# A mixture-of-experts stage: TensorE's order taken from the program, transposes at fixed places, a GpSimd drain for each expert

## The chip, the core and the metric

One core of one Trainium2 chip runs the whole program. The metric is the device time of one execution in microseconds (us), median of several runs. The engines are TensorE (PE; its weight loads are listed apart as PEld), VectorE (DVE), ScalarE (ACT), GpSimd (POOL) and SyncE (SP, which here only issues DMAs).

## The reference

Three layers follow one another: attention among clustered tokens, a dense MLP, and a mixture of experts over the MLP's output. Only the last layer is touched:

```
def _moe2_ref(x, w_gate, w_noise, noise, w1, w2):       # x: 1536 x 512, E = 8 experts, F = 1024
    noisy_logits = x @ w_gate + log1p(exp(x @ w_noise)) * noise
    top2, top2_w = two largest per token, softmax over the two
    for e in range(E):
        for k in range(2):
            mask = top2[:, k] == e
            h = maximum(x[mask] @ w1[e], 0)
            out[mask] += top2_w[mask, k, None] * (h @ w2[e])
```

## The kernel before

Attention and the MLP take the first two thirds of the time. While the MLP's second half runs (`middle`, line 1237), tokens are routed: each token's row is scattered to a slot list in DRAM, `xs`, one region per expert. Then `moe2` (line 1427) works through the experts in passes. One call of `expert` (line 1380) is one pass over some slots of one expert:

- Pass A is expert 1, first half (240 slots); pass B expert 0, second half; pass C expert 1, second half. (Expert 0's first half is in `middle`.)
- Six passes follow, one for each other expert, in order of load; they are called here by their slots: R432, R416, R408, R400, R392 and R384.

**A pass.** `ffn1` (lines 1320 to 1338) multiplies the first weights with the transposed rows `xT`, 12 matmuls into PSUM bank 0 or 1 for each of eight blocks `fb` of the hidden layer; ACT writes the high part `hh` (relu), DVE the rest `hl`. `ffn2` (line 1340; `ffn2_t`, line 1372, with the operands the other way round) adds that block's share to the pass's accumulators: three matmuls for each of two, three or four banks from bank 2 on. The program's loop is ffn1 one block ahead of ffn2. For the last three blocks (`TAIL`), ffn2 comes at the end, accumulator by accumulator, so that an accumulator is ready after each three groups of three matmuls. This stretch is called the tail: 6 groups with two accumulators, 12 with four.

**The result.** Passes R432 to R392 are "flipped": the accumulators hold the result transposed, ACT and DVE alternately copy them to `yT`, and during the next pass four "back" steps (function `after`) transpose them on TensorE through PSUM banks 6 and 7 in turn; DVE scales them (`put`, line 1358), and POOL scatters them to `out` by an indirect DMA. A pass whose `Y` is true adds to rows that an earlier pass wrote, so POOL clears `Y` and gathers the old rows (`gather_out`, line 1207: a memset and one indirect DMA per accumulator).

**The next pass's rows.** `xpose_part` (line 1226), called four times, transposes a fourth of the next rows `X` into bank 6 or 7 (the two in turn), ACT copies it to `xT` (line 1234), and DVE writes the low part (line 1235). So the third call can't write its bank before ACT and DVE have read the first call's. `meta` (line 1175) works out six small things from `X` on POOL.

**The next weights.** In each pass eight pieces of weights are prepared (`conv`): SP loads a 512 KB piece into one of three buffers `stg`, ACT makes the high part (line 1127), DVE and for some pieces POOL the low part (line 1131); when a piece is done, its buffer takes the piece after next but one. The `step` hook places them: pieces 0 to 7 of a pass after its blocks 0 to 7.

**What sets the order.** The framework's planner orders each engine's queue by its own model of times. `manual_schedule` exempts engines from that: their queue is in the program's order. For `moe2` this is said of ACT and SP (lines 1579 and 1580), and for TensorE only in the tail of the last pass. So in every other place of `moe2`, TensorE's order is the planner's. POOL's and DVE's is the planner's throughout. `last()` in the tail of a pass fetches and transposes the next rows.

Of the kernel before, what the change touches and what calls it, by code (L numbers as in the profile page):

```python
# [14 lines left out]
AF = mybir.ActivationFunctionType  # L15
# [8 lines left out]
DM = H * D  # L24
KB = DM // 128
# [4 lines left out]
FB2 = F2 // 128  # L30
# [4 lines left out]
CH = HALF // 2  # L35
# [10 lines left out]
TAIL = 3  # L46
# [54 lines left out]
PRI = 600  # L101
PRI1 = 600
FX = FB1 - KB
OOB = 1.0e6
TINY = float(2.0 ** ((897 + 128) // 8 - 127) * (1 + ((897 + 128) % 8) / 8))
NP = H // 2
# [508 lines left out]
class Moe:  # L615
# [7 lines left out]
    def consts(self):  # L623
# [27 lines left out]
        nc.vector.memset(z[:, DM + 2:DM + 3], -1.0)  # L651
        nc.vector.memset(z[:, DM + 3:DM + 4], OOB)
        self.zrow = z
# [510 lines left out]
    def gather_half(self, b):  # L1164

        X = (self.rows if b else self.yp).tile([CH, 2, 2, ROW], F32, tag="R" if b else "Y", name="Xh")
        for e in range(2):
# [20 lines left out]
    def gather_rest(self, e, r):  # L1188
# [6 lines left out]
                       allow_small_or_imprecise_dtypes=True)  # L1195
        v.tensor_scalar(sl[:, :, 1:2], sl[:, :, 0:1], t[:, 3:4], OOB, op0=OP.is_ge, op1=OP.mult)
        v.scalar_tensor_tensor(sl[:, :, 1:2], sl[:, :, 0:1], t[:, 0:1], sl[:, :, 1:2], op0=OP.is_lt, op1=OP.mult)
# [9 lines left out]
    def gather_out(self, g):  # L1207
        nc = self.nc
        m, idx = g
        Y = self.yp.tile([m.shape[0], m.shape[1], DM], F32, tag="Y", name="Y")  # L1210
        nc.gpsimd.memset(Y, 0.0)
        for k in range(m.shape[1]):
            nc.gpsimd.indirect_dma_start(
                out=Y[:, k, :], out_offset=None, in_=self.out,
                in_offset=bass.IndirectOffsetOnAxis(ap=idx[:, k, 0:1], axis=0),
                bounds_check=NT - 1, oob_is_err=False)
        return Y

# [121 lines left out]
    def ffn2(self, W, ps, h, fb, ks=None):  # L1340
        nc = self.nc
        hi, lo = W[FB2 + fb]
        hh, hl = h
        for k in range(len(ps)) if ks is None else ks:
            cp = ps[k].shape[0]
            sl = slice(k * cp, (k + 1) * cp)
            for n, (a, w) in enumerate(((hh, hi), (hh, lo), (hl, hi))):
                nc.tensor.matmul(ps[k], a[:, sl], w, start=(fb == 0 and n == 0), stop=(fb == FB2 - 1 and n == 2))

    def combine(self, g, Y):  # L1350
        nc, tc = self.nc, self.tc
# [25 lines left out]
            for n, (w, a) in enumerate(((hi, hh), (lo, hh), (hi, hl))):  # L1377
                self.nc.tensor.matmul(ps[d], w[:, sl], a, start=(fb == 0 and n == 0), stop=(fb == FB2 - 1 and n == 2))  # L1378

    def expert(self, W, xT, g, Y, cp, last=lambda: None, before=lambda: None, final=False, flip=False,  # L1380
               step=lambda i: None):

        nc = self.nc
        ck = xT.shape[3] // cp
        if flip:
            ffn2, ps = self.ffn2_t, [self.bank((2 + d,), [128, ck * cp]) for d in range(KB)]
        else:
            ffn2, ps = self.ffn2, [self.bank((2 + k,), [cp, DM]) for k in range(ck)]
        h = [self.ffn1(W, xT, 0)]
        for fb in range(FB2 - TAIL):  # L1390
            h.append(self.ffn1(W, xT, fb + 1))
            if fb == 0:
                before()
                Y = self.gather_out(g) if Y else None
                if final:
                    self.tc.keep_in_program_order(nc.gpsimd.drain())
            ffn2(W, ps, h[fb], fb)
            step(fb)
        for fb in range(FB2 - TAIL + 1, FB2):
            h.append(self.ffn1(W, xT, fb))  # L1400
            step(fb - 1)
        put = self.combine(g, Y)
        yT = self.xg.tile([128, KB, ck * cp], F32, tag="xU", name="yT") if flip else None
        with self.tc.manual_schedule(engines={mybir.EngineType.PE}) if final else ExitStack():
            for k in range(len(ps)):
                if k == len(ps) // 2:
                    last()
                    step(FB2 - 1)
                for fb in range(FB2 - TAIL, FB2):
                    ffn2(W, ps, h[fb], fb, (k,))  # L1410
                if not flip:
                    put(k, ps[k])
                elif k % 2:
                    nc.vector.tensor_copy(yT[:, k], ps[k])
                else:
                    nc.scalar.activation(yT[:, k], ps[k], AF.Copy)

        def after():
            for k in range(ck if flip else 0):
                pt = self.bank((6, 7), [cp, DM])  # L1420
                for d in range(KB):
                    nc.tensor.transpose(pt[:, d * 128:d * 128 + 128], yT[:, d, k * cp:(k + 1) * cp], self.ident)
                put(k, pt)

        return after

    def moe2(self, W0, W1, xT1, m1):

        nxt = [None, None]
        n, W, X, reg, st = {}, {}, {}, {}, {}  # L1430
        pieces = [(e, s) for e in range(2, E) for s in ORDER]
        count = {"ld": 0, "cv": 0}

        def second():
            nxt[:] = self.gather_half(1)
            self.xpose(*nxt[0][:2], (6, 7))

        def load():
            i = count["ld"]
            if i == len(pieces):  # L1440
                return
            count["ld"] += 1
            e, s = pieces[i]
            if s == ORDER[0]:
                reg[e] = self.nc.values_load(self.ordi[0:1, e - 2:e - 1], engines=(mybir.EngineType.SP,), min_val=2,
                                             max_val=E - 1)
                W[e] = [None] * 8
            st[i] = self.weights_load(s, [w[bass.ds(reg[e], 1)].rearrange("o k n -> (o k) n")
                                          for w in (self.w1, self.w2)])

        def conv():
            i = count["cv"]
            if i == len(pieces):
                return
            count["cv"] += 1
            e, s = pieces[i]
            W[e][s] = self.weights_split(e % 2, st.pop(i), s)
            load()

        def rows(e):  # L1460
            X[e] = self.gather(reg[e], *CAPS[e - 2])

        def turn(e):
            cp, ck = CAPS[e - 2]
            n["xT"] = self.xtile(cp * ck)
            self.xpose(X[e], n["xT"], (6, 7))
            n["m"] = self.meta(X.pop(e)[:, :, DM:], self.ord[:cp, e - 2:e - 1], self.nc.gpsimd)

        def plan(e, at):
            def step(i):  # L1470
                if i == at[0]:
                    rows(e)
                if i in at[1]:
                    conv()
            return step

        def first(i):
            if i == FB2 - 1:
                for _ in range(3):
                    load()  # L1480

        self.expert(W1, xT1, m1, True, CH, second, step=first)
        self.expert(W0, nxt[0][1], nxt[0][2], False, CH, lambda: self.xpose(*nxt[1][:2], (6, 7)),
                    step=plan(2, (4, (3, 5, 7))))
        done = lambda: None
        self.expert(W1, nxt[1][1], nxt[1][2], True, CH, lambda: turn(2), step=plan(2, (None, (0, 2, 3, 5, 6))))
        for e in range(2, E):
            xT, m = n["xT"], n["m"]
            more = e + 1 < E
            done = self.expert([x for p in W.pop(e) for x in p], xT, m, True, CAPS[e - 2][0],  # L1490
                               lambda: turn(e + 1) if more else None, done, not more, more,
                               plan(e + 1, (0, range(FB2))) if more else lambda i: None)

    def rest(self):
# [12 lines left out]
def kernel(ctx, tc, q, k, v, centroids, moe_w_in, moe_w_out,  # L1507
                                                         w_gate, w_noise, noise, w1, w2, out):
    nc = tc.nc
# [40 lines left out]
    def hook(fb):  # L1550
        if fb % 2:
            s["W"] += moe.weights_part(0, 0, fb // 2, (w1[0], w2[0]))
        if 1 <= fb <= NB:
            next(run)
        elif fb == FX:
            s["A"] = moe.gather_half(0)
        if fb >= FX:
            for X, xT, _ in s["A"]:
                moe.xpose_part(X, xT, fb - FX, (0, 1))
        yield  # L1560
# [15 lines left out]
    bctx.close()  # L1576
    moe.wB = pool(ctx, "c_wB", 1)
    W1 = moe.middle(acc, s["W"], *s["A"][0][1:], (w1[1], w2[1]))
    with tc.manual_schedule(engines={mybir.EngineType.Activation, mybir.EngineType.SP}):
        moe.moe2(s["W"], W1, *s["A"][1][1:])  # L1580
    moe.rest()

# [30 lines left out]
```

## Time and profile before

| | us |
|---|---|
| median of 3 runs | 921.78 (921.45 to 922.41) |
| the profiled execution's own time | 922.68 |
| its span, first to last instruction | 920.9 |
| TensorE busy | 881.6 (96%) |
| VectorE busy | 572.5 (62%) |
| ScalarE busy | 487.1 (53%) |
| GpSimd busy | 398.3 (43%) |

Busy time is the union of the engine's instructions as the hardware profiler recorded them. The profiled execution's own time holds 1.8 us that lie outside its span. All time stamps are us from the start of the span.

### The profile page before, as it was taken

The numbers are of one execution on the slowest core, as the hardware profiler recorded it, in microseconds if no ns is written. First come the engines' busy times: TensorE is split into PE (matmuls) and PEld (weight loads), VectorE is DVE, ScalarE is ACT, GpSimd is POOL, SyncE is SP. The second block draws the span as 40 slices with busy tenths as digits, with TensorE's granted clock in tenths as the row PEclk, the third lists the DMA queues.
The fourth block names the chain that finished last, engine by engine and source line by source line (L and its number), as shares of the span: only waits on it lengthen the run. The fifth ranks groups of instructions, "written<-read, shape, count | busy, mean of one in ns | idle before, by whom it ended". The sixth has DMA issues, their size and how long they took to land. (4 is left out here: it accounts for less than half of the span.)

```text
span 920.9 us, 14876 instructions
## 1 busy us (share of the span) xinstructions
PE 881.6 (96%) x5277; PEld 806.0 (88%) x5277; DVE 572.5 (62%) x1129; ACT 487.1 (53%) x1021; POOL 398.3 (43%) x459
## 2 busy tenths in 40 slices
PE   6999999999898999999999999989999999999996
PEld 4898998989887888889998988978879999999995
DVE  3889989998996676676446654652533525445431
ACT  2788888878795565565335444521433324434320
POOL 3134434443565989881000421163432254464631
PEclk9899999999999999999999999999999999999999
DMA  8756765676522333412100340273564455556511
GB/s 216 186 136 181 188 160 163 165 216 180 151 71 101 116 115 115 138 47 69 46 23 24 126 124 23 70 232 115 165 170 128 145 160 168 155 164 198 164 37 65
DMA packets 77531, 120.13 MB, mean 130 GB/s; under 512 B 9858, under 2 KB 55939, under 8 KB 76941
## 3 DMA queue, kind: packets, MB, share of 16 engines
q1 hardware_dynamic: 69997, 100.98, 37.8%
q0 software_dynamic: 7456, 18.16, 6.3%
q8 instruction: 43, 0.70, 0.3%
q14 instruction: 35, 0.29, 0.1%
HBM read 72.85 MB, written 23.76 MB: 105 GB/s over the span
## 5 line engine op out<-in xcount | busy, mean ns | idle before, releaser
L1334 DVE SCALAR_TENSOR_TENSOR hl<-bank,hh 128x240 fp32r<-128x240 f32 (+6 forms) x80 | 40.4, 509 | 138.0 <-ACT hh L1333 138.0
L1333 ACT ACTIVATE hh<-bank 128x240 fp32r<-128x240 f32 (+6 forms) x80 | 35.4, 453 | 169.4 <-PE bank L1325 169.4
L435 DVE TENSOR_TENSOR PTl<-ps_pt,PTh 128x384 fp32r<-128x384 f32 x192 | 98.5, 548 | 12.0 <-ACT PTh L430 11.0
L430 ACT ACTIVATE PTh<-ps_pt 128x384 fp32r<-128x384 f32 x192 | 87.7, 497 | 28.9 <-PE ps_pt L420 27.8
L403 DVE TENSOR_REDUCE nm<-ps_s 128x1 f32<-128x768 f32 x96 | 91.1, 949 | 13.9 <-PE ps_s L398 13.5
L420 PE MATMUL ps_pt<-ident,P 128*128 128x128 f32 x576 | 87.9, 276 | 3.9 <-DVE PTl L435 3.5
L411 ACT ACTIVATE P<-ps_s,nm 128x768 f32<-128x768 f32 x96 | 87.3, 910 | 5.0 <-DVE nm L403 5.0
L1325 PE MATMUL bank<-xT,wB 128*128 128x240 f32 (+3 forms) x480 | 83.7, 321 | 0.0
L420 PEld LDWEIGHTS ps_pt<-ident,P 128*128 128x128 f32 x576 | 68.3, 141 | 13.9 <-DVE PTl L435 10.7
L1325 PEld LDWEIGHTS bank<-xT,wB 128*128 128x128 f32 x480 | 77.2, 192 | 2.2
L823 PE MATMUL bank<-woh,gh 128*128 128x512 f32 x192 | 76.1, 396 | 0.0
L823 PE MATMUL bank<-wol,gh 128*128 128x512 f32 x192 | 75.0, 391 | 0.0
L397 PE MATMUL ps_s<-k,q 128*128 128x384 f32 x192 | 70.7, 368 | 0.7 <-DMA k<-ABk 0.3
L823 PE MATMUL bank<-woh,gl 128*128 128x512 f32 x192 | 69.9, 391 | 0.0
L398 PE MATMUL ps_s<-k,q 80*128 80x384 f32 x192 | 66.7, 347 | 3.1 <-DMA nzt<-in_moe_noise_dram 3.1
L1131 POOL TENSOR_TENSOR wA<-stg,wA 128x512 fp32r<-128x512 f32 x16 | 20.6, 1292 | 107.9 <-DVE wol L715 54.1
L1363 POOL DMA_INDIRECT out_dram<-Y,idx x31 | 35.1, 1133 | 58.6 <-DVE Y L1362 30.0
L455 PE MATMUL ps_o<-PTh,vs 128*128 128x256 f32 x288 | 53.8, 295 | 0.6 <-ACT PTh L430 0.3
L455 PE MATMUL ps_o<-PTl,vs 128*128 128x256 f32 x288 | 53.6, 295 | 0.0
L1325 PE MATMUL bank<-xT,wA 128*128 128x240 f32 (+3 forms) x300 | 51.2, 319 | 0.0
L1378 PE MATMUL bank<-hh,wA 128*128 128x432 f32 (+2 forms) x192 | 50.4, 354 | 0.2 <-ACT hh L1333 0.2
L1325 PEld LDWEIGHTS bank<-xT,wA 128*128 128x128 f32 x300 | 48.0, 189 | 1.4
(311 smaller groups left out, 2301.8 us busy)
## 6 DMA issues: line engine op xcount, KB each, us to landing
stg<-in_moe_w_dram SPq DMA_DIRECT2D x64, 512.0 KB
q<-ABq SPq DMA_DIRECT2D x48, 192.0 KB
k<-ABk SPq DMA_DIRECT2D x48, 192.0 KB
si<-in_moe_w_in_dram SPq DMA_DIRECT2D x14, 512.0 KB
so<-in_moe_w_out_dram SPq DMA_DIRECT2D x14, 512.0 KB
xs<-zrow SPq DMA_DIRECT2D x24, 217.7 KB
ld<-in_k_dram SPq DMA_DIRECT2D x8, 384.0 KB
ld<-in_q_dram SPq DMA_DIRECT2D x8, 384.0 KB
```

The source lines that it names most:

```text
L397: self.nc.tensor.matmul(o, self.g("S1", u, "q")[:, h, qs], self.g("S1", u, "k")[:, h, ks], start=True, stop=False)
L398: self.nc.tensor.matmul(o, self.g("S2", u, "q")[:80, h, qs], self.g("S2", u, "k")[:80, h, ks], start=False, stop=True)
L403: self.nc.vector.tensor_reduce(nm, self.g("s", j)[:, :, :384], axis=AX.XY, op=OP.max, negate=True)
L411: self.nc.scalar.activation(P, self.t.pop(("s", j))[:, :, :384], AF.Exp, bias=self.t.pop(("nm", j)), scale=1.0, accum_out=self.g("sums", u ...
L420: self.nc.tensor.transpose(ps[:, k, :], P[:, k * 128:(k + 1) * 128], self.ident)
L430: self.nc.scalar.activation(self.pt_at(j, g, 0), self.g("pt", j, g), AF.Copy)
L435: self.nc.vector.tensor_sub(self.pt_at(j, g, 1), self.t.pop(("pt", j, g)), f(self.pt_at(j, g, 0)))
L455: self.nc.tensor.matmul(self.g("O", u, qp)[:, h, :], vs[:, h, 2 * i + half].rearrange("p a d -> p (a d)"), PTx[:, kc, :], start=(c == 1 an ...
L823: nc.tensor.matmul(acc[j], g[:, sl], w, start=(fb == 0 and n == 0), stop=(fb == FB1 - 1 and n == 2))
L1325: self.nc.tensor.matmul(ps, w[:, kb, :], xT[:, kb, x], start=(kb == 0 and i == 0), stop=(kb == KB - 1 and i == 2))
L1334: self.nc.vector.scalar_tensor_tensor(hl, ps, 0.0, f(hh), op0=OP.max, op1=OP.subtract)
L1378: self.nc.tensor.matmul(ps[d], w[:, sl], a, start=(fb == 0 and n == 0), stop=(fb == FB2 - 1 and n == 2))
```

## The change

TensorE joins ACT and SP in `manual_schedule` for all of `moe2`, so the places of its instructions in the program become its order. The program is therefore written out more finely. The parts of the next rows' transposes are handed over as a list, and each stands behind a numbered group of the tail (`AT`; pass A has a list of its own, `LATE`). The four back steps of the pass before stand one by one ahead of and behind ffn2 of blocks 0 and 1 (`turn`). `gather_out` is called when the last of them is done; where there are such steps, a `drain` of POOL stands ahead of it. Before, there was one drain, in the last pass, behind `gather_out`. The hook's step 7 comes with the last transposed part, and `meta` ahead of the first. The passes with a drain are R416, R408, R400, R392 and R384.

```
+AT = {2: (1, 2, 3, 4), 3: (), 4: (3, 4, 6, 7)}
+LATE = (3, 4, 5, 5)
...
+        turns = list(before)
+
+        def turn():
+            nonlocal Y
+            if turns:
+                turns.pop(0)()
+            if Y is True and not turns:
+                if before:
+                    self.tc.keep_in_program_order(nc.gpsimd.drain())
+                Y = self.gather_out(g)
+            elif not Y:
+                Y = None
+
         h = [self.ffn1(W, xT, 0)]
         for fb in range(FB2 - TAIL):
             h.append(self.ffn1(W, xT, fb + 1))
-            if fb == 0:
-                before()
-                Y = self.gather_out(g) if Y else None
-                if final:
-                    self.tc.keep_in_program_order(nc.gpsimd.drain())
+            turn()
             ffn2(W, ps, h[fb], fb)
+            turn()
             step(fb)
...
-        with self.tc.manual_schedule(engines={mybir.EngineType.PE}) if final else ExitStack():
-            for k in range(len(ps)):
-                if k == len(ps) // 2:
-                    last()
+        groups = [(k, fb) for k in range(len(ps)) for fb in range(FB2 - TAIL, FB2)]
+        at = at or AT[len(ps)]
+        nxt, n = None, 0
+        for i, (k, fb) in enumerate(groups):
+            ffn2(W, ps, h[fb], fb, (k,))
+            while n < len(at) and at[n] == i:
+                if n == 0:
+                    nxt = last()
+                if n < len(nxt):
+                    nxt[n]()
+                n += 1
+                if n == len(at):
                     step(FB2 - 1)
-                for fb in range(FB2 - TAIL, FB2):
-                    ffn2(W, ps, h[fb], fb, (k,))
...
+        def back(k):
+            pt = self.bank((6, 7), [cp, DM])
+            for d in range(KB):
+                nc.tensor.transpose(pt[:, d * 128:d * 128 + 128], yT[:, d, k * cp:(k + 1) * cp], self.ident)
+            put(k, pt)
+
+        return [lambda k=k: back(k) for k in range(ck if flip else 0)]
...
+        def parts(X, xT):
+            return [lambda kb=kb: self.xpose_part(X, xT, kb, (6, 7)) for kb in range(KB)]
+
         def second():
             nxt[:] = self.gather_half(1)
-            self.xpose(*nxt[0][:2], (6, 7))
+            return parts(*nxt[0][:2])
...
-            self.xpose(X[e], n["xT"], (6, 7))
-            n["m"] = self.meta(X.pop(e)[:, :, DM:], self.ord[:cp, e - 2:e - 1], self.nc.gpsimd)
+            n["m"] = self.meta(X[e][:, :, DM:], self.ord[:cp, e - 2:e - 1], self.nc.gpsimd)
+            return parts(X.pop(e), n["xT"])
...
-        self.expert(W1, xT1, m1, True, CH, second, step=first)
+        self.expert(W1, xT1, m1, True, CH, second, step=first, at=LATE)
...
-    with tc.manual_schedule(engines={mybir.EngineType.Activation, mybir.EngineType.SP}):
+    with tc.manual_schedule(engines={mybir.EngineType.PE, mybir.EngineType.Activation, mybir.EngineType.SP}):
         moe.moe2(s["W"], W1, *s["A"][1][1:])
```

## Rows read from the trace of the kernel before

**Rows 1.** The profile's page, part 1: busy time, share of the span, instructions.
```profile
PE 881.6 (96%) x5277; PEld 806.0 (88%) x5277; DVE 572.5 (62%) x1129; ACT 487.1 (53%) x1021; POOL 398.3 (43%) x459
```
**Rows 2.** Waits of TensorE, 575 to 914 us: total, times, longest.
```profile
PE bank L1232 <- DMA Xh<-xs: 4.3, 1, 4.3
PE bank L1232 <- DMA X<-xs: 1.9, 1, 1.9
PE bank L1325 <- ACT xT L1234: 1.5, 1, 1.5
PE bank L1348 <- ACT hh L1333: 0.2, 1, 0.2
```
**Rows 3.** Stretches behind two long waits; PEclk, the granted clock, is third from the end.
```profile
622.80:626.20 3.40, 3.40 (x15) 3.13 (x14) 0.00 (x0) 0.13 (x1) 2.91 (x6) 0.50 1.06 312
762.80:766.10 3.30, 3.30 (x13) 3.13 (x12) 1.19 (x3) 1.37 (x4) 0.00 (x0) 0.50 0.57 157
```
**Rows 4.** TensorE in order of time: start, duration, what, [idle before <-releaser].
```profile
604.09 1.08 PE L1348 MATMUL bank<-wB,hh 128*120 128x512 f32 x4
...
605.47 1.50 PE L1325 MATMUL bank<-xT,wB 128*128 128x240 f32 x12
606.81 1.10 PE L1348 MATMUL bank<-wB,hh 128*120 128x512 f32 x4
...
622.24 0.53 PE L1232 MATMUL bank<-ident,Xh 120*128 120x120 f32 x3 [4.32 <-DMA Xh<-xs]
...
686.14 0.90 PE L1232 MATMUL bank<-ident,X 104*128 104x104 f32 x8 [1.85 <-DMA X<-xs]
686.82 1.09 PE L1378 MATMUL bank<-hl,wA 128*128 128x432 f32 x4
687.71 4.04 PE L1325 MATMUL bank<-xT,wg 128*128 128x432 f32 x12
...
698.65 2.52 PE L1325 MATMUL bank<-xT,wA 128*128 128x432 f32 x12
...
785.70 2.40 PE L1325 MATMUL bank<-xT,wA 128*128 128x408 f32 x12
787.93 0.53 PE L1378 MATMUL bank<-hh,wA 128*128 128x408 f32 x2
...
790.15 2.38 PE L1325 MATMUL bank<-xT,wA 128*128 128x408 f32 x12
```
**Rows 5.** ScalarE in order of time, at the ends of passes R416 and R408.
```profile
759.22 1.15 ACT L1127 ACTIVATE wA<-stg 128x512 fp32r<-128x512 f32 x2 [6.14 <-DMA stg<-in_moe_w_dram]
...
799.56 1.16 ACT L1127 ACTIVATE wB<-stg 128x512 fp32r<-128x512 f32 x2 [3.88 <-DMA stg<-in_moe_w_dram]
...
801.01 0.89 ACT L1234 ACTIVATE xT<-bank 128x400 fp32r<-128x400 f32 x2
```
**Rows 6.** GpSimd in order of time, passes R416 (first row) and R408.
```profile
738.60 0.31 POOL L1180 TENSOR_SCALAR m<-X,ord 102x4 f32<-102x4 f32 x1 [8.19 <-DMA X<-xs]
...
780.52 1.34 POOL L1363 DMA_INDIRECT out_dram<-Y,idx  x1 [0.30 <-DVE hl L1334]
...
784.12 1.81 POOL L1211 MEMSET Y<- 102x2048 f32 x1 [0.92 <-DMA out_dram<-Y,idx]
...
791.89 1.30 POOL L1131 TENSOR_TENSOR wx<-stg,wx 128x512 fp32r<-128x512 f32 x1
```
**Rows 7.** DMAs issued by SP, in order of time.
```profile
726.04 0.32 SPq L1161 DMA_DIRECT2D X<-xs  x1
...
793.21 0.37 SPq L1118 DMA_DIRECT2D stg<-in_moe_w_dram  x1
```
**Rows 8.** By line: the one drain; the gathers' time to landing; the last gather.
```profile
L1396 POOLq DRAIN  x1: 9335/9335/9335, 896.7 to 896.7; - x1
...
DMA to landing us min/median/max: 3.3/4.0/5.9
...
898.48 1.00 POOL L1213 DMA_INDIRECT Y<-out_dram,idx  x1 [0.30 <-issue]
```

More of the change, by code (lines that the diff above doesn't have):

```diff
@@ L1378, in ffn2_t, with expert @@
                 self.nc.tensor.matmul(ps[d], w[:, sl], a, start=(fb == 0 and n == 0), stop=(fb == FB2 - 1 and n == 2))
-    def expert(self, W, xT, g, Y, cp, last=lambda: None, before=lambda: None, final=False, flip=False,
-               step=lambda i: None):
+    def expert(self, W, xT, g, Y, cp, last=lambda: [], before=(), final=False, flip=False,
+               step=lambda i: None, at=None):
         nc = self.nc
@@ L1401, in expert @@
             step(fb - 1)
+        assert not turns
         put = self.combine(g, Y)
         yT = self.xg.tile([128, KB, ck * cp], F32, tag="xU", name="yT") if flip else None
-        with self.tc.manual_schedule(engines={mybir.EngineType.PE}) if final else ExitStack():
-            for k in range(len(ps)):
-                if k == len(ps) // 2:
-                    last()
-                    step(FB2 - 1)
-                for fb in range(FB2 - TAIL, FB2):
-                    ffn2(W, ps, h[fb], fb, (k,))
[L1411 to L1425, printed above, removed]
+        groups = [(k, fb) for k in range(len(ps)) for fb in range(FB2 - TAIL, FB2)]
[10 more added lines that the diff above has]
+                if n == len(at):
+                    step(FB2 - 1)
+            if fb < FB2 - 1:
+                continue
+            if not flip:
+                put(k, ps[k])
+            elif k % 2:
+                nc.vector.tensor_copy(yT[:, k], ps[k])
+            else:
+                nc.scalar.activation(yT[:, k], ps[k], AF.Copy)
+        def back(k):
[4 more added lines that the diff above has]
+        return [lambda k=k: back(k) for k in range(ck if flip else 0)]
     def moe2(self, W0, W1, xT1, m1):
@@ L1480, in first @@
                     load()
-        self.expert(W1, xT1, m1, True, CH, second, step=first)
-        self.expert(W0, nxt[0][1], nxt[0][2], False, CH, lambda: self.xpose(*nxt[1][:2], (6, 7)),
+        self.expert(W1, xT1, m1, True, CH, second, step=first, at=LATE)
+        self.expert(W0, nxt[0][1], nxt[0][2], False, CH, lambda: parts(*nxt[1][:2]),
                     step=plan(2, (4, (3, 5, 7))))
-        done = lambda: None
+        done = ()
         self.expert(W1, nxt[1][1], nxt[1][2], True, CH, lambda: turn(2), step=plan(2, (None, (0, 2, 3, 5, 6))))
@@ L1490, in moe2 @@
             done = self.expert([x for p in W.pop(e) for x in p], xT, m, True, CAPS[e - 2][0],
-                               lambda: turn(e + 1) if more else None, done, not more, more,
+                               lambda: turn(e + 1) if more else [], done, not more, more,
                                plan(e + 1, (0, range(FB2))) if more else lambda i: None)
```

## The prediction

> **What bounds the kernel now.** I read the busy times first: TensorE is busy 96% of the span [rows 1]. In the expert passes that hides two things: the waits of TensorE, and the speed at which it runs behind them. So the second view is the waits of TensorE from pass A to the end of the last pass [rows 2]. Four kinds are long enough to count, and three of them are single waits: 4.3 us for the rows `Xh`, 1.9 us for the rows `X`, 1.5 us for `xT` from ScalarE. The rest is 0.2 us apiece. The third view is the granted clock behind them [rows 3]: after the first and the third wait it stands at 0.50, the 1.2 GHz level, for about 3.4 us, with TensorE busy all the time. Behind the second, twelve matmuls take 4.04 us where the same twelve take 2.52 in the same pass later [rows 4], so that one is slowed too. Half speed for 3.4 us costs 1.7 us. The short waits of 0.2 us have no such stretch that I count.
>
> Where the waits stand is seen in TensorE's queue in order of time [rows 4]. At 617.92 (622.24 less 4.32) the planner has put transposes of the next rows ahead of pass A's last ffn1 block; the rows land 4.3 us later, while that block and six groups, which need no new rows, stand behind them. At 684.3 it has put R416's transposes at the start of R432, a whole pass early. Both are faults of order alone. The third is not: there ScalarE itself waited 6.14 us for a weight piece [rows 5], and everything in its fixed queue behind that, `xT` too, came late. R408's end shows the same, 3.88 us, with no wait of TensorE at that place.
>
> **The change part by part.** *Added and removed work.* TensorE has the same matmuls and transposes; ACT, DVE and SP the same instructions. Four drains are added on POOL, and one is moved. So the sum consists of waits.
>
> *First wait.* In the program's order TensorE goes on at 617.92 with ffn1 of block 7, 1.34 us (605.47 to 606.81), then four groups; two groups take 1.38 (604.09 to 605.47), so four take 2.76 [rows 4]. The first transpose is reached at 622.02, the rows are there at 622.24: 0.2 us remain of 4.32, and I take it that the clock holds, as I see no slow stretch behind waits of 0.2. The parts that follow lie behind groups 4 and 5, as 240 columns on ACT and DVE need less time than a group and its transposes. Saved: 4.1 + 1.7. SP's fetch of `Xh` moves in the program, but SP has nothing else to issue in between, so it keeps its time.
>
> *Second wait.* R416's rows have landed by 686.14, and their transposes now stand in R432's tail, nearly 30 us later. Saved: 1.85 + 1.7.
>
> *Third wait and the tails of R416, R408, R400 and R392.* Saved if nothing takes its place: 1.5 + 1.7. But now the third part of the transposes stands in the tail behind group 6, and its bank is free only when ACT and DVE have read the first part. ACT's copy stands behind piece 6 of the weights, and that piece's load goes out when POOL has finished piece 3, which it does behind `gather_out` [rows 6, 7]. So I follow one such pass, R408's size, from its start. One ffn1 block takes 2.23 us, ffn2 of four groups 2.22 (785.70, 787.93, 790.15), eight transposes 0.68 [rows 4], so one back step 0.34. The last back step ends after five blocks and four steps: 11.1 + 1.4 = 12.5. Its put and hand-over are 1.0 (an estimate: two ACT passes over 512 columns take 1.16 [rows 5]). The last scatter starts at 13.5; the memset came 3.6 later (780.52 to 784.12), POOL's low part 7.8 after that, and takes 1.3 [rows 6]: 26.2. From the issue of the load to ScalarE's start is 6.35 (793.21 [rows 7] to 799.56 [rows 5]); from there to `xT` 1.45 [rows 5]; reading the first part to the end about 1.05 (half of 0.89, and as much again for DVE): 35.05. TensorE comes to the third part after thirteen blocks, four back steps, seven groups and two parts: 28.9 + 1.4 + 3.9 + 0.7 = 34.9. So it waits some 0.15 us. The chain is that much earlier than in before because there the last scatters stood behind `meta`, and `meta` waited for `X`: 8.19 us in R416 [rows 6].
>
> *The drain.* It stands on POOL between the last scatter and the memset; behind it wait the memset, the gathers, POOL's low parts, thereby SP's loads and ScalarE. The memset waits for the scatter's landing anyhow, so a drain that only waits for landings costs nothing. The one drain of before is on record with 9.34 us from 896.7, to 906.0; the last gather ahead of it was issued at 898.48 and landed, by the median of 4.0, at 902.5 [rows 8], so it held POOL 3.5 us beyond. Bounds: nothing and 3.5 us for each pass. That drain was the first, behind 79 indirect transfers; a new one comes behind eight since the last drain. Taken by transfers, 3.5 x 8 / 79 is 0.35. I take that, as the gathers themselves follow one another without such holds. So three passes (R408, R400, R392) wait 0.15 + 0.35 each: 1.5 together. In R384 no transposes and no weight pieces follow, and its gathered rows are first used at the end of the pass, so its drain is covered there.
>
> The Trainium skill has a rule against this reading: "Perfetto Trace Analysis", section "Sequencer-only Instruction (DRAIN, etc)", says that the profile's record of a drain is its execution alone, without any wait for semaphores ahead of it. By it the whole 9.34 us would be the drain's own, four times on this chain, and the time about 940. The trace does not bear that out as a price: a gather starts at 898.48, inside the drain's record.
>
> *R416.* It has the first drain, and the slowest rows: 12.6 us from issue (726.04 [rows 7]) to landing (738.60 [rows 6]). The fetch comes about 1.5 us into the pass (an estimate: it stands in SP's queue behind the load that follows piece 7, now prepared with the last transposes). If the planner leaves `meta` ahead of the last two scatters, the last one starts at 1.5 + 12.6 + 1 + 1.4 = 16.5, not 13.5: 3.0 us more, and 1.7 for the clock. So between 0.5 and 5.2; neither is nearer to a row, and I take the middle, 2.9.
>
> **Sum.** 922.68, the profiled execution's own time, less 6.0 (first), 3.55 (second) and 3.2 (third) is 909.9. Back come 0.2, 1.5 and 2.9: 914.5. The runs' median lies 0.9 below that execution: 913.6.
>
> **The rivals.** *A new wait in place of the old.* The planner may leave POOL's chain as late as it was. Then the first part is read 2.5 us after piece 6 is begun: at 761.7 in R416, 802.1 in R408 [rows 5]. Five groups (2.8) before the tails' ends, about 759.7 and 802.0, TensorE stands before the third part: waits of 4.8 and 2.9, and R400's I take as R408's. That is 10.6 and three times 1.7, so 909.9 + 0.2 + 15.7 - 0.9 = 924.9. For it: ACT's queue is the same as before, and POOL's is still the planner's. Against it: the scatters no longer have to stand behind late rows, as these are fetched sooner. *Slower by the drain.* If each drain holds POOL its full 9.3, the memset comes 5.7 later than 3.6 in four passes: each waits about 5.9 and loses 1.7, 30 in all: about 940. The drains and their waits eat the whole gain from 1.4 us of wait a pass on (12.5 / 4, less 1.7). For it is the one record; against it that its gathers ran inside. *Part of the gain.* All four tails wait about a microsecond, with half speed behind: 909.9 + 0.2 + 4 x 2.7 - 0.9 = 920.0.
>
> **How the numbers follow.** A measurement of this kernel tells 0.2%, 1.8 us, from no change. Forecast 0.60, with a range of its own from 908.8 (no new waits, 909.9 - 0.9, rounded down) to 917.5 (two tails at their upper bounds); part of the gain 0.12; the new wait 0.16; the drain 0.12. Faster: all of the first and two thirds of the second, 0.68. Same: the rest of the second and half of the third, 0.12. Slower: 0.20. The range from 908.8 to 925 leaves out the drain's case and a little at either end.
>
> **What would show it.** In the new profile the waits for `Xh` and `X` should be gone from TensorE's list (0.2 at most for `Xh`), with the half-speed stretches at 623 and 688. At the ends of R416 to R392 the transposes should stand as four parts between groups, with a short wait or none ahead of the third. On POOL the scatters should come before `meta`, and each drain should end within half a microsecond of the last scatter's landing. I am wrong if ScalarE still waits 4 us or more for piece 6: then TensorE waits for `bank` in the tails, and if the drains reach microseconds past the landings, all of it turns to a loss.

## The result: 0.8% slower, and the profile after

The changed kernel takes 929.0 us (median of 12 runs, 923.43 to 932.06), the kernel before 921.05 on the same chip (12 runs, 917.14 to 923.91). The ratio is 1.0081, 95% interval 1.0062 to 1.0101. The forecast was 913.6 with a range up to 925: wrong in sign.

The profiled execution took 930.48 us, its span is 928.6. The page's first part and the waits of TensorE, 575 to 925 us, answer [rows 1] and [rows 2]. The columns of the second are total, times, longest.

```profile
PE 879.4 (95%) x5277; PEld 802.3 (86%) x5277; DVE 571.7 (62%) x1129; ACT 488.4 (53%) x1021; POOL 393.3 (42%) x459
```
```profile
PE bank L1234 <- DVE xT L1237: 8.6, 5, 3.9
PE bank L1350 <- ACT hh L1335: 7.0, 1, 7.0
PE bank L1380 <- ACT hh L1335: 0.3, 1, 0.3
PE bank L1380 <- DVE hl L1336: 0.3, 1, 0.3
```

Up to line 1390 every line stands two further down than before: transposes are L1234, ACT's and DVE's parts of `xT` L1236 and L1237, ffn1 L1327, ffn2 L1350 and L1380, the put L1364. TensorE's busy time is what it was. The waits for `Xh`, `X` and `xT` from ScalarE are gone, as the change meant. In their place stand waits for a bank that DVE's low part of `xT` has not yet read, and one wait of 7.0 us for ScalarE's `hh` in pass A. Their sum is 16 us, where before had 8.

TensorE in order of time shows the three long ones, which answer [rows 4]: in pass A, at pass A's end, and ahead of the third part in R408's tail.

```profile
619.06 1.21 PE L1350 MATMUL bank<-wx,hh 128*120 128x512 f32 x2 [7.02 <-ACT hh L1335]
...
634.28 0.42 PE L1234 MATMUL bank<-ident,Xh 120*128 120x120 f32 x2 [1.81 <-DVE xT L1237]
...
801.36 0.93 PE L1234 MATMUL bank<-ident,X 100*128 100x100 f32 x4 [3.95 <-DVE xT L1237]
```

Stretches behind the first and the last of them, as [rows 3] (granted clock third from the end): 1.2 GHz again, 0.50 of full speed.

```profile
619.10:622.40 3.30, 3.30 (x10) 2.68 (x10) 2.50 (x22) 0.17 (x1) 0.00 (x0) 0.50 0.15 25
...
801.40:806.70 5.30, 5.30 (x20) 5.08 (x21) 2.66 (x5) 2.44 (x5) 1.03 (x1) 0.50 0.33 102
```

The five drains, by line, answer [rows 8]: minimum, median and maximum, first and last start.

```profile
L1399 POOLq DRAIN  x5: 3606/5006/7826, 734.0 to 898.7; - x5
```

### The profile page after: what moved, and what is told of

Same layout as the page of the kernel before. It is cut to its first block, busy times and chain, and to the rows that moved or that the text cites. A ratio compares the mean times of both kernels' runs of the same rounds, so it can differ in the third digit from the quotient of the medians.

```text
span 928.6 us, 14870 instructions
## 1 busy us (share of the span) xinstructions
PE 879.4 (95%) x5277; PEld 802.3 (86%) x5277; DVE 571.7 (62%) x1129; ACT 488.4 (53%) x1021; POOL 393.3 (42%) x459
## 5 line engine op out<-in xcount | busy, mean ns | idle before, releaser
L1327 PE MATMUL bank<-xT,wB 128*128 128x240 f32 (+3 forms) x480 | 79.7, 318 | 0.0
L1327 PEld LDWEIGHTS bank<-xT,wB 128*128 128x128 f32 x480 | 75.9, 189 | 1.8
L1380 PE MATMUL bank<-hh,wA 128*128 128x432 f32 (+2 forms) x192 | 54.3, 365 | 0.0
L1327 PE MATMUL bank<-xT,wA 128*128 128x240 f32 (+3 forms) x300 | 50.8, 320 | 0.0
L1327 PEld LDWEIGHTS bank<-xT,wA 128*128 128x128 f32 x300 | 47.8, 189 | 1.3
```

Source lines behind the costliest of these rows:

```text
L1327: self.nc.tensor.matmul(ps, w[:, kb, :], xT[:, kb, x], start=(kb == 0 and i == 0), stop=(kb == KB - 1 and i == 2))
```

## The experiments

### Both kernels once more: what belongs to the kernel and what to one execution

The 7.0 us looked odd: TensorE had ended the block that `hh` reads 9.3 us before ScalarE began it, and no other wait stood in ScalarE's queue. So the changed kernel was run again unchanged (`e1_again`), and later the kernel before (`e8_before_again`).

> The changed kernel as it is, once more. In its first profile TensorE waits 7.0 us in pass A for ScalarE's hh of block 5, though TensorE had ended that block 9.3 us earlier and no other wait stands in ScalarE's queue; records of DMA landings are thin there. Theory 'the order makes it': the wait comes from the new order and stands in every execution; then it is here again at about 7 us, and TensorE's waits from 575 us on sum to about 16 us. Rival 'of that one execution': the wait is gone or elsewhere, the waits sum to about 9 us, and the time of the profiled execution is below 925 us. In either case the tails of R416, R408, R400 and R392 wait for the bank of the third part by about 1, 4, 1.4 and 0.5 us.

> The kernel before as it is, once more, for a second trace: the waits for Xh (4.3), X (1.9) and xT (1.5) should stand at the same places, each with a stretch of half clock, if they belong to the kernel and not to the one execution shown.

`e1_again`: 926.56 us against 918.16 of the kernel before on that chip, ratio 1.0093 (1.0057 to 1.0129); profiled 927.09, span 925.3. `e8_before_again`: one run of 917.46 us, span 915.6. The waits of TensorE in the changed kernel, then in the kernel before:

```profile
PE bank L1234 <- DVE xT L1237: 11.7, 4, 6.1
PE bank L1380 <- DVE hl L1336: 1.0, 1, 1.0
```
```profile
PE bank L1232 <- DMA Xh<-xs: 3.9, 1, 3.9
PE bank L1232 <- DMA X<-xs: 1.5, 1, 1.5
PE bank L1325 <- DVE xT L1235: 0.3, 1, 0.3
PE bank L1348 <- ACT hh L1333: 0.2, 1, 0.2
PE bank L1378 <- ACT hh L1333: 0.2, 1, 0.2
```

Neither theory for the changed kernel held whole. The wait for `hh` is gone, so it is not a part of every execution (what caused it stays open). But the wait at pass A's fourth part, 1.81 us in the first trace, is now 6.15 (630.34). In the kernel before, the wait of 1.5 us for `xT` is not there the second time. Its median was 921.05 us beside the first trace and is 917.15 on the chip of the second, so whether the first trace's extra waits belong to one execution or to its chip is not shown. Granted clocks: three stretches of the kernel before (behind `Xh`, behind `X`, and R408's start, whose counterpart in [rows 3] has 0.50), then two of the changed kernel (behind 6.15 us in pass A, behind 2.84 in R408).

```profile
622.10:624.90 2.80, 2.80 (x12) 2.60 (x13) 0.00 (x0) 0.00 (x0) 2.60 (x8) 0.50 1.06 240
686.00:689.40 3.40, 3.40 (x22) 3.28 (x22) 0.00 (x0) 0.00 (x0) 3.21 (x8) 1.00 0.43 151
...
757.50:760.90 3.40, 3.40 (x23) 3.07 (x22) 2.17 (x5) 1.49 (x5) 0.58 (x1) 1.00 0.46 164
```
```profile
630.40:636.50 6.10, 6.10 (x28) 5.99 (x29) 1.67 (x4) 1.08 (x3) 2.10 (x2) 0.50 0.23 63
800.40:803.80 3.40, 3.40 (x14) 3.18 (x13) 2.03 (x4) 2.36 (x5) 0.30 (x1) 0.50 0.58 159
```

These two traces (of two chips) account for the loss. Waits: 11.7 + 1.0 against 3.9 + 1.5 + 0.3 + 0.2 + 0.2, 6.6 us more. Half speed: 6.1 + 3.4 against 2.8 us, of which half is lost, 3.3 more. Together 9.9 us; the spans differ by 9.7 (925.3 less 915.6).

### Pass A: a put in DVE's queue

In `e1_again` pass A's end reads so on TensorE, DVE and GpSimd:

```profile
623.82 0.37 PE L1234 MATMUL bank<-ident,Xh 120*128 120x120 f32 x2
630.34 0.66 PE L1234 MATMUL bank<-ident,Xh 120*128 120x120 f32 x2 [6.15 <-DVE xT L1237]
```
```profile
622.82 0.41 DVE L1237 TENSOR_TENSOR xT<-bank,xT 128x240 fp32r<-128x240 f32 x1 [2.88 <-ACT xT L1236]
629.22 0.75 DVE L1364 SCALAR_TENSOR_TENSOR Y<-bank,m,Y 120x512 f32<-120x512 f32 x1 [5.99 <-DMA Y<-out_dram,idx]
629.88 0.40 DVE L1237 TENSOR_TENSOR xT<-bank,xT 128x240 fp32r<-128x240 f32 x1
```
```profile
622.75 0.94 POOL L1213 MEMSET Y<- 120x1024 f32 x1
...
624.04 1.15 POOL L1215 DMA_INDIRECT Y<-out_dram,idx  x1 [0.19 <-POOL m L1186]
625.50 1.09 POOL L1215 DMA_INDIRECT Y<-out_dram,idx  x1 [0.30 <-issue]
```

The fourth part needs the bank of the second. DVE's low part of the second needs 0.40 us, but in DVE's queue, which is the planner's, the put of the first accumulator stands ahead of it. That put adds to gathered rows `Y`, which land at 629.1. So DVE stands for 5.99 us, and TensorE behind it. The Trainium skill says of it ("PSUM — Partial Sum Buffer", section "Engine vs sequencer instructions") that the queues of ScalarE, VectorE and GpSimd are strict FIFO; the trace agrees, with a ready 0.40 us instruction behind a waiting one for 6 us.

In the kernel before (`e8_before_again`) the same put waits for the same rows, at 629.93. But there the planner had ordered two low parts ahead of it, and it filled TensorE's time with tail groups and with the next pass's ffn1:

```profile
626.52 0.71 DVE L1235 TENSOR_TENSOR xT<-bank,xT 128x240 fp32r<-128x240 f32 x2
629.93 1.56 DVE L1362 SCALAR_TENSOR_TENSOR Y<-bank,m,Y 120x512 f32<-120x512 f32 x2 [2.69 <-DMA Y<-out_dram,idx]
```

Three runs test this: the planner's order in pass A alone (`e2_passA`), the gathers sooner (`e6_gather_first`), and the put later (`e7_put_last`). Their edits, shortened:

```
e2  -    with tc.manual_schedule(engines={PE, Activation, SP}):
    +    with tc.manual_schedule(engines={Activation, SP}):      # in moe2, from pass B on: {PE}
e6  +        with self.tc.manual_schedule(engines={mybir.EngineType.Pool}):
                 self.expert(W1, xT1, m1, True, CH, second, step=first, at=LATE)
e7  +        if at is LATE:                                       # the tail of pass A
    +            stack.enter_context(self.tc.manual_schedule(engines={mybir.EngineType.DVE}))
             ...
    +            if at is LATE: held.append(k)                    # in place of put(k, ps[k])
             ...
    +        for k in held:                                       # behind groups and parts
    +            put(k, ps[k])
```

> The changed kernel, but TensorE's order is the planner's in pass A, and the program's from pass B on. If the first wait of the changed kernel (7.0 us in pass A, and 1.8 for the fourth part) is made by the program's order there: the old wait for Xh of about 4.3 us with 1.7 for the clock comes back in its place, some 4.5 us less in all, about 924.5. If the 7.0 us belong to one execution and not to the order: the old wait comes back for the 1.8 us alone, 4 us more, about 933.

> The changed kernel with GpSimd too in the program's order during pass A: memset and gathers of the old rows Y stand ahead of meta, which waits for Xh. In pass A's tail TensorE waits 6.2 us for the bank that DVE's low part reads, DVE stands in the put, and the put waits 6.0 us for these gathers. If the gathers' late start is the cause: memset at about 620.3 instead of 622.8, the rows 2.5 to 3.7 us sooner, the wait 6.2 falls to 2.5 to 3.7, and with less at half clock some 3 to 5 us off. If the wait has another cause (the part's place), it stays at 6 us.

> The changed kernel with DVE's two puts of pass A behind the four low parts of xT (DVE in the program's order in that tail). If DVE's order is what turns the late gathers into a wait of TensorE: the wait of 6.2 us for the fourth part goes; pass B starts its two blocks of ffn1 (2.9 us), and then ffn2 waits about 2.5 us for the accumulator that the put frees at about 630. So 3.5 us less, and 1 to 2 for the clock. If the low parts wait for something else, the 6 us stay.

`e2_passA`: 927.58 us, ratio 1.0104 (1.0068 to 1.0139), no different from `e1_again`: the wait for `Xh` is back (4.5), the 6.15 gone. Expected were 924.5 or 933, so neither came. The time does not tell what pass A's order alone is worth: in this trace pass A loses less than in `e1_again` (waits of 4.5 and 0.5 and 1.7 for half speed, against 6.15 and 3.1), but R416's third part waits 4.3 where `e1_again` has 1.5.

`e6_gather_first`: 925.46, ratio 1.0077 (1.0058 to 1.0096). The first gather was issued at 622.82, 1.2 us sooner, and the put still waited to 629.25; TensorE's wait was 6.7. That GpSimd's order makes the rows late has fallen, as far as 1.2 us can tell: 2.5 were meant, but the memset had to wait for the scatters ahead of it. The gathers took 6.3 and 5.7 us from issue to landing, where `e1_again` has 5.0 and 4.3.

```profile
621.57 0.96 POOL L1213 MEMSET Y<- 120x1024 f32 x1 [4.46 <-DMA out_dram<-Y,idx]
622.82 1.12 POOL L1215 DMA_INDIRECT Y<-out_dram,idx  x1 [0.30 <-POOL Y L1213]
```

`e7_put_last`: 920.04 against 917.15, ratio 1.0040 (1.0018 to 1.0061), 0.53% below `e1_again`, and 5.4 us below `e6_gather_first` on the same chip. It is the largest single piece of the loss, and it goes by one engine's order alone. The low parts now run as the parts come, the put waits from then on, and TensorE waits for it only at pass B's first ffn2, by 3.0 us where 2.5 were expected:

```profile
PE bank L1234 <- DVE xT L1237: 4.5, 3, 2.8
PE bank L1350 <- DVE Y L1364: 3.0, 1, 3.0
```

### The drains

Edits: `if before:` ahead of the drain becomes `if final:` (`e3_no_drains`); a drain ahead of `gather_out` in the kernel before, in the same five passes (`e4_drains_only`).

> The changed kernel with the drain in the last pass alone; GpSimd's queue is else the same. Theory 'the drains': in the changed kernel the drains end 5.9, 5.4, 4.8 and 4.4 us after the issue of the last scatter in R416 to R392, where the memset of before starts 3.6 after it; without them the memset, the low parts, SP's loads and ScalarE come 2.3, 1.8, 1.1 and 0.8 us earlier and the waits of the third parts shrink by as much, from 1.0, 4.0, 1.4 and 0.5 to 0, 2.2, 0.2 and 0: 4 us less, and 1.7 to 2.7 for the clock if R408's wait becomes short, so 923 to 925. Rival 'the places of the parts': the tails wait since the parts stand too early, with drains or without; the memset waits for the last scatter's landing anyhow, the waits stay within 0.5 us, and so does the time, 929.

> The kernel before with the drains alone: one ahead of gather_out in R416 to R384, the planner's order of TensorE kept (GpSimd's first low part of a pass moves from ahead of the memset to behind it). Theory 'the drains': the chain from the last scatter to ScalarE's piece 6 is 1 to 2 us longer in each pass, plus 1.3 for the low part; R416's wait for xT grows from 1.5 to 3 to 5 us, R408 gets a wait of up to 3 us, so 923 to 929. Rival 'the places of the parts': drains alone are covered, since the planner sets the transposes at the end of the tail: within 1 us of before, 921 to 922.

`e3_no_drains`: 924.11 where `e1_again` has 926.56, ratio 1.0061 (1.0039 to 1.0082). `e4_drains_only`: 922.38 where the kernel before has 918.16, ratio 1.0049 (1.0031 to 1.0068); in its trace R416's wait for `xT` is 3.1 us, R408 and R400 get 0.4 and 0.8. (Its profiled execution took 926.89 us, the slowest of the twelve.) So the drains cost 2.5 us in the changed kernel and 4.2 alone, where each pass's first low part of GpSimd (1.3 us) also moved behind the memset. The 4.2 are clear of no change; the 2.5 are less so, as the intervals of `e3_no_drains` and `e1_again` overlap, and in the trace the tails' waits fall only from 6.5 to 5.3 us, R408's not at all (3.7). That the drains are covered has fallen; that they are the main cause too. From the last scatter's issue to the memset, in us:

| | R416 | R408 | R400 | R392 | R384 |
|---|---|---|---|---|---|
| before (`e8_before_again`) | 3.2 | 3.5 | 5.0 | 3.8 | 3.1 |
| changed (`e1_again`) | 6.3 | 5.6 | 5.1 | 4.3 | 3.6 |
| changed, one drain in R384 (`e3_no_drains`) | 4.2 | 5.5 | 4.5 | 3.9 | 7.5 |

These differences hold more than the drain, since the last scatter takes 3.0 to 5.4 us to land, by pass and run. Its landing is in the trace too, and from there to the memset it is, in us:

| | R416 | R408 | R400 | R392 | R384 |
|---|---|---|---|---|---|
| before (`e8_before_again`), no drain between | 0.1 | 0.1 | 0.1 | 0.1 | 0.1 |
| changed (`e1_again`), a drain in each | 2.1 | 0.6 | 0.6 | 0.6 | 0.6 |
| before with drains (`e4_drains_only`) | 2.1 | 0.6 | 0.6 | 0.6 | 0.6 |
| changed, one drain in R384 (`e3_no_drains`) | 0.1 | 0.1 | 0.1 | 0.1 | 4.5 |

So a drain that follows another by one pass adds about 0.45 us, R416's, the first, 1.9, and R384's, where it is the only one, 4.3.

### The tails: two fixed places

R408 in `e1_again`, ahead of the third part. GpSimd, SP, ScalarE, and TensorE:

```profile
775.50 1.00 POOL L1365 DMA_INDIRECT out_dram<-Y,idx  x1 [0.39 <-DVE Y L1364]
781.14 1.82 POOL L1213 MEMSET Y<- 102x2048 f32 x1 [4.65 <-DMA out_dram<-Y,idx]
782.92 1.36 POOL L1133 TENSOR_TENSOR wB<-stg,wB 128x512 fp32r<-128x512 f32 x1
...
790.48 1.29 POOL L1133 TENSOR_TENSOR wx<-stg,wx 128x512 fp32r<-128x512 f32 x1
```
```profile
791.80 0.37 SPq L1120 DMA_DIRECT2D stg<-in_moe_w_dram  x1
```
```profile
797.14 1.15 ACT L1129 ACTIVATE wB<-stg 128x512 fp32r<-128x512 f32 x2 [4.39 <-DMA stg<-in_moe_w_dram]
...
798.58 0.89 ACT L1236 ACTIVATE xT<-bank 128x400 fp32r<-128x400 f32 x2
```
```profile
799.74 0.56 PE L1234 MATMUL bank<-ident,X 100*128 100x100 f32 x4 [2.84 <-DVE xT L1237]
```

It is the chain that the prediction followed, later by 3 us. In `e8_before_again` the planner put the third and fourth parts where TensorE waited for neither, within the next pass's first block, which needs them last:

```profile
796.73 0.54 PE L1325 MATMUL bank<-xT,wB 128*128 128x400 f32 x2
797.11 0.51 PE L1232 MATMUL bank<-ident,X 100*128 100x100 f32 x4
797.39 1.34 PE L1325 MATMUL bank<-xT,wB 128*128 128x400 f32 x6
798.57 0.51 PE L1232 MATMUL bank<-ident,X 100*128 100x100 f32 x4
```

`e5_later_parts` moves the two parts four groups back:

```
-AT = {2: (1, 2, 3, 4), 3: (), 4: (3, 4, 6, 7)}
+AT = {2: (1, 2, 3, 4), 3: (), 4: (3, 4, 10, 11)}
```

> The changed kernel with the third and fourth part of the transposes behind groups 10 and 11 of a four-bank tail instead of 6 and 7. In the kernel before, the planner had let these parts slip behind the whole tail of R408, into the next pass's first block, which needs them last. If the fixed places 6 and 7 make the waits of the tails: the waits of about 1, 1.4, 2.8 and 1.3 us (once more run) shrink by the four groups, 2.2 us, to near nothing, R408's to at most 1; about 0.5 us a pass comes back as a wait for xT in the next block; 5 us less with the clock, some 921 against 926.5 on the same chip. If they only move: the tails' sums stay within 1 us, and so does the time.

925.02 us, ratio 1.0076 (1.0054 to 1.0098). In the trace R408's wait of 2.8 became 0.7 (for `hl`), but R416's became 1.1 + 0.3 + 2.7; the tails' sum is 5.8 us against 6.5, within the 1 us of the rival. The places alone give at most 1 or 2 us, which these intervals do not tell from nothing, and less than I expected. A part that stands later also delays what is behind it: piece 7, SP's next load, and with it the next fetch of `X`, which in R416 is issued 3.9 us into the pass where `e1_again` has 1.4.

### Taken together

> Two edits together: pass A's puts behind the low parts, and the drain in the last pass alone. If pass A's put and the drains are two separate causes, their gains add: 6.5 and 2.5 us off the changed kernel, 917.5, the time of the kernel before. If both act through the same wait, no more than the 920.0 of the first alone.

> The same two edits, and the third and fourth parts behind groups 10 and 11. Theory 'the fixed places are the third cause': the tails' waits of 1.0, 2.8 and 0.7 us in R416, R408 and R400 go but for about 0.5 each, 2 to 3 us less and 1.7 for the clock where R408's wait was followed by half speed: 913 to 915.5. Rival 'they only move' (in the run with later parts R416's wait grew from 1.0 + 1.5 to 1.1 + 2.7, with the rows X fetched later): within 1 us of the run with two edits.

> The three edits, and pass A's three weight loads (512 KB each) issued ahead of the fetch of Xh instead of behind it. With GpSimd's gathers of Y moved 1.2 us forward they landed no sooner; if that is because the weights' transfers run at the same time, then now Y lands 2 to 3 us sooner, and the wait of ffn2 for the put in pass B (3.0 us) shrinks by as much. If the gathers' 4 to 5 us are their own, the wait stays at 3 us. The price may be a later Xh: the scatters ahead of it share the queues with the weights.

> The three edits (without the loads), and the fetch of the next rows X one place earlier in SP's queue, ahead of the load that follows piece 7 of the pass before. In the changed kernel GpSimd's meta, ahead of three of the four scatters, waits 3.4, 2.0, 0 and 0.9 us for X in R416 to R392. If meta's wait sets when the scatters end, and so the memset, the low parts and ScalarE's piece 6: the waits of meta go, R416's tail gets 1 to 3 us of room, and the time falls by up to 2 us. If the landing of the scatters or the loads sets it: no change.

The kernel before has 917.81 beside these. `e9_put_last_no_drains` (the edits of e7 and e3): 917.11, ratio 0.9993 (0.9976 to 1.0009). The two causes add, and with both taken away the change is worth nothing: in this trace TensorE still waits 4.8 us in the tails and 2.9 for the put, where the kernel before waited 3.9 for `Xh` and 1.5 for `X`. `e10_and_later_parts` (with e5's too): 917.84, 0.9998 (0.9984 to 1.0013), the rival's outcome. `e11_loads_ahead` (`first` loads at `i == FB2 - 2`): 916.62, 0.9993 (0.9976 to 1.0010); the put's wait went, and a wait of 3.3 us for `Xh`, issued at 621.30 instead of 616.8, came in its place. The gathers did land faster: from issue to landing, in `e10_and_later_parts` and then in `e11_loads_ahead`:

```profile
DMA to landing us min/median/max: 4.7/5.0/5.3
DMA to landing us min/median/max: 3.5/3.7/3.8
```

So over 1 us of their time came from the loads beside which they ran. The last three scatters into `xs`, which the fetch of `Xh` waits for, paid for it: they took 7 to 8 us to land, where `e10_and_later_parts` has 3.2 to 3.7. They do not stand in the loads' queue, as the expectation had it (the profile lists q0 for GpSimd's transfers and q1 for SP's); it gives both as a share of the same 16 DMA engines.

`e12_rows_ahead` fetches `X` ahead of piece 7's load:

```
-        def plan(e, at):
+        def plan(e, at, ahead=E):
             def step(i):
                 if i == at[0]:
                     rows(e)
+                if i == FB2 - 1 and ahead < E:
+                    rows(ahead)
                 if i in at[1]:
                     conv()
```

(In its calls, `ahead` is the pass after the next.) 914.83 us, ratio 0.9978 (0.9965 to 0.9992): the only version that beats both kernels, the one before by 0.2%. `X` is issued 0.3 us into R416, where `e10_and_later_parts` had 3.9. `meta` still waits 8.1 us for it, so the expectation that its waits go was wrong, but it starts 4 us earlier in the pass. TensorE's waits are down to these:

```profile
PE bank L1350 <- DVE Y L1364: 3.0, 1, 3.0
PE bank L1380 <- DVE hl L1336: 0.9, 1, 0.9
PE bank L1234 <- DVE xT L1237: 0.7, 1, 0.7
```

## Why the prediction was wrong

**First wait (6.0 us saved): this step failed.** It said that the parts lie behind groups 4 and 5, "as 240 columns on ACT and DVE need less time than a group and its transposes". That was right as far as it goes (ACT's copy takes 0.37 us, DVE's low part 0.40). What stood between them on DVE was not looked at: the put, and behind the put the gathers. The old wait of 4.3 us lay in front of a later one for rows that land at about 629 in either order. In place of 4.3 + 1.7 the changed kernel has 6.15 + 3.05 (`e1_again`). No rival had this place; the one of a new wait in place of the old had only the tails, at 4.8, 2.9 and 2.9 us where `e1_again` has 1.5, 2.8 and 1.3 ahead of the third parts.

**Third wait (3.2 us) and the clock behind the second (1.7): these stood in one trace of two.** The prediction took them from the profiled execution and corrected only by 0.9 to the median. In the second trace of before neither is there: 1.5 us of wait for `X` at full clock, none for `xT` from ScalarE. Of the 12.75 us of saving (6.0 + 3.55 + 3.2), 4.9 (3.2 + 1.7) were not there to save in the second trace.

**Second wait (1.85):** right; it is gone in both traces of the changed kernel.

**R408's tail (0.15 + 0.35): mis-sized by 2.3.** From the pass's start (761.35 in `e1_again`) the last scatter came at 14.2, not 13.5; the memset 5.6 later, not 3.6 + 0.35, as the scatter took 5.1 to land, not 3.4; the low part 9.3 after that, not 7.8, as the pass's first low part had moved between. It ended at 30.4 instead of 26.2 + 0.35. A shorter load gave 1 us back (5.3 from issue to ScalarE, not 6.35). TensorE reached the third part at 35.5 (predicted 34.9) and waited 2.84, and half speed behind it cost 1.7 more, for which the sum had nothing. R416's 2.9 was about right in size (2.4 in `e1_again`, but only 1.5 of it ahead of the third part; 1.0 is ffn2's wait for `hl`), R400's 0.5 is 1.25.

**The drains (0.35 each): nearly right in R408, R400 and R392** (0.45 each, by the landings), and 1.9 in R416, which the prediction had left inside R416's own bounds. The Trainium skill's rule in "Perfetto Trace Analysis", section "Sequencer-only Instruction (DRAIN, etc)", that a drain's record is its execution alone, does not give its price here: the records are 5.0 us in the median, but each begins ahead of the last scatter's and holds the wait for its landing, and removing four of them gave 2.5 us in all.

**What would have shown it** was named rightly for the tails (waits for `bank`), and not for pass A.

## What to carry to other kernels

A wait removed is worth the distance to the next one, so ask of each engine that serves the moved work what stands in its queue between the pieces, and what that waits for: here a put on DVE, whose rows landed 6 us later, undid a saving that TensorE's queue alone seemed to promise. When one engine's order is fixed by hand and the order of the engine that serves it is left to a planner, the two can come to stand against each other; `e7_put_last` took away over half of the loss with DVE's order alone. And a saving read from one profiled execution is worth checking in a second: over a third of this one was not in the second.

## What the runs showed that I had not expected

- A drain's price grew with the indirect transfers issued since the last one: the memset starts 0.6 us behind the last scatter's landing with eight or nine of them, 2.1 with 42 or 43 (R416), 4.5 with 75 (R384 of `e3_no_drains`), and 0.1 without a drain.
- A wait of the same length is followed by half speed in one run and not in another. In R408 2.84 us of wait is followed by 0.50 for 3.4 us in `e1_again`; behind 2.84 us at the same place in `e7_put_last` the clock is 1.00:

```profile
794.70:798.10 3.40, 3.40 (x22) 3.17 (x23) 2.67 (x5) 2.31 (x5) 0.18 (x1) 1.00 0.60 159
```
- In the first trace of the changed kernel ScalarE began `hh` 9.3 us after TensorE's last matmul for it, with nothing else recorded that it waited for. `e1_again`, `e3_no_drains` and `e5_later_parts` share pass A's order and have nothing like it; the cause is open.
- The gathers of pass A land at about 629 in each order. Two runs bear on it: issued 1.2 us sooner they took as much longer (`e6_gather_first`), and with the weight loads ahead they took 3.5 to 3.8 us, not 4.7 to 5.3 (`e11_loads_ahead`). So the loads hold them up; how much of the rest is their own is open.
